# One attention-and-expert kernel: batch 0's token reads taken from the opening to mid-run, and the whole hand-written order of the work set anew

## The chip, the cores and the metric

The kernel runs on one core of a Trainium2 chip. The metric is the device time of one execution in microseconds (us). Three runs of the kernel before took 211.06, 211.47 and 211.60 us; their median, 211.47 us, is its time. A fourth run was profiled; every row quoted below comes from it.

## What is computed

Eight batches of tokens `x` (8 heads, 512 tokens, 64 features) and states (8 heads, 32 rows, 64 features) read each other, and the results go through one layer with a leaky activation. Cut from the reference:

```python
scores  = scale * x @ state.T            # tokens read states
a       = softmax(scores)                # over the 32 states
xread   = a @ state
scores2 = scale * state @ x.T            # states read tokens
a2      = softmax(scores2)               # over the 512 tokens
sread   = a2 @ x
y = concat([xread, sread])               # 8 x 544 rows of 512
h = y @ w_in                             # 512 -> 2048
g = maximum(h, 0) + alpha * minimum(h, 0)
out = g @ w_out                          # 4352 x 512, float32
```

## The kernel before

**The order.** No loop and no scheduler sets the order. One string, ORDER, lists tokens such as `F.1.4.5`, and each token calls one step. A step issues a few instructions, and every engine runs its instructions in the order in which the string brings them. What a step needs it waits for by semaphores. So a place in the string is a place in up to five queues at once: TensorE (PE), VectorE (DVE), ScalarE (ACT), GpSimd (POOL) and SyncE (SP), the last two of which issue the DMAs. A trailing number is one of the PSUM banks k0 to k5; scores and a few other results use a two-bank buffer, called "two" here. An engine letter (a, v, p) chooses ACT, DVE or POOL.

**Tokens read states, then the first matrix.** The weights `a` stay apart from the states: the states go through `w_in` at once (step m, L521: eight matmuls for each batch and 512 columns; mo, L545 and L547, brings the result to SBUF), and the transposed weights are multiplied by that (F, L570: two 128x512 matmuls fill one bank `h`; batch 0 has a few quarters f, L592). For batch b the weights come by this chain: scores sc (L314, PE), turned into blocks sb (L346, DVE), their maximum smax (L379, DVE), subtracted by ssh (L384, POOL), exponent sexp (L393, ACT), sum and reciprocal ssum (L400, L401, DVE), division snorm (L404, DVE, for batch 0 POOL), turned back wb (L412, DVE). Batch 0's weights come from a second set of scores with tokens in rows (tsc, L353) and are turned on PE (at, L365).

**The activation.** N (L623, ACT) reads the bank and writes the negative part; G (L626, DVE) reads both and writes `g` in half precision. The bank is free when G is done. A bank `h` thus takes PE, ACT and DVE in turn.

**The second matrix.** Batch 0 uses plain matmuls (S, L640; O, L657). Batches 1 to 7 and the state rows, called batch 8, use products of halves (P, L728, four 128x256 matmuls each) on sums of `w_out` (W, L683, POOL) and of `g` (U, L707, POOL or DVE); K (L744) keeps a product, Q (L759, L761) adds it and issues the output's DMA from SP.

**States read tokens.** From the same scores: the maximum tm (L424, DVE), its negative nb (L431 ACT or L433 DVE), two exponents te (L441, ACT), reciprocals tsum (L451, DVE). Two steps tn (L457 ACT or L459 POOL) divide the exponents, tt (L463) turns them by a DMA on SP (`e2T`), rd (L475, PE) multiplies them with `x`, rdo (L486, ACT) takes the reads out of PSUM. Four batches' reads are turned together (rt, L494) and later fill batch 8, whose first matrix is L579.

**Loads.** POOL's queue carries the four parts of `w_in` (wi, L207), the four of `w_out` (wo, L213), the states of batches 1 to 7 (lst, L201) and `x` of batches 1 to 7 (lx, L161), which casts to half precision; three buffers `xg` hold `x` in turn. Batch 0's `x` comes by SP in float32 and is cast (L172, L177); batch 0's states come by ACT in float32 (L185). `x` of batches 0 and 1 is turned on PE (xt, L299, out by xo, L304), that of the others by a DMA on SP (xd, L291, `xT`). Fills (Z, L232) are matmuls on a pattern, whose result nobody reads.

Of the kernel before, what the change touches and what calls it, by code (L numbers as in the profile page):

```python
# [8 lines left out]
F32 = mybir.dt.float32  # L9
F16 = mybir.dt.float16  # L10
# [7 lines left out]
Z.1.1 Z.2.1 stc.a cx.0.0.a stt.3 wi.0 sbd.0.a Z.4.1 cx.0.1.v xt.0.0.1.5 xo.0.0.1.a sbd.1.v xt.0.0.0.0 xo.0.0.0.v  # L18
tsc.0.1.1 lst cx.1.0.a lx.1 sto.a cx.1.1.v tsc.0.0 Z.2.1 wi.1 smax.0.0 xt.0.1.1.4 xo.0.1.1.v xt.0.1.0.5 wo.0 tsc.1.1.0
xo.0.1.0.a tsc.1.0 Z.2.1 m.0.0.3.4 ssh.v.0.0 sc.0.1 sexp.0.0 oma wi.2 mo.0.0.a.0 mo.0.0.a.1 Z.5.1 smax.0.1 ssum.0.0  # L20
snorm.p.0.0 ssh.v.0.1 str.0.1 sro.0.a sc.0.0 tm.0 Z.2.1 sexp.0.1 str.1.5 Z.3.1 at.0.4 ao.0.v nb.0.v ssum.0.1
xt.1.1.1.2 xo.1.1.1.v sro.1.a m.4.0.0.1 mo.4.0.v.0 te.0.1 te.0.0 xt.1.1.0.3 xo.1.1.0.a xt.1.0.1.4 f.0.1.0.5 mo.4.0.v.1
m.1.0 mo.1.0.v f.0.0.0.2 n.0.1.0 snorm.p.0.1 xt.1.0.0.0 at.1.1 ao.1.v n.0.0.0 xo.1.0.1.a g.0.1.0.0 g.0.0.0.1 m.0.1.3.1
xo.1.0.0.a sc.1 m.2.0.4.0 mo.0.1.a.1 mo.0.1.a.0 mo.2.0.a.0 g.0.0.0.0 S.0.2.0.1 mo.2.0.a.1 tm.1 sb.1 F.0.5.2 F.0.4.3
nb.1.a wo.1 g.0.1.0.1 wi.3 f.0.1.1.4 N.0.5 G.0.5 F.0.6.0 te.1.0 smax.1 N.0.4 S.0.2.1 G.0.4 F.0.7.5 te.1.1 f.0.0.1.2
m.0.2 N.0.6 n.0.1.1 G.0.6 g.0.1.1.1 mo.0.2.a g.0.1.1.0 wo.2 wo.3 tsum.0 S.0.1.2.3 S.0.2.2 F.0.11.0 N.0.7 G.0.7 ssh.p.1
n.0.0.1 F.0.10.4 g.0.0.1.0 g.0.0.1.1 S.0.1.1 N.0.11 G.0.11 sexp.1 ssum.1.5 m.0.3 mo.0.3.a S.0.2.3 S.0.1.3 S.0.1.0
m.1.1 N.0.10 G.0.10 tn.0.0.p mo.1.1.a tn.0.1.p tt.0 F.0.9.2 snorm.v.1 F.0.8.0 N.0.8 m.1.3 N.0.9 G.0.9 S.0.1.5 mo.1.3.a
W.1.0.p F.0.14.4 N.0.14 F.0.15.5 N.0.15 S.0.2.5 m.1.2 mo.1.2.a G.0.8 S.0.2.4 wb.1 lx.2 G.0.14 xd.2 F.0.13.2 N.0.13
# [12 lines left out]
N.2.8 G.2.8 N.2.1 F.2.13.4 K.1.2.a G.2.1 N.2.13 P.1.7.0.0.2 G.2.13 P.1.7.1.1 m.3.3.1.3 ssh.p.3 m.2.1 sexp.3 tn.2.1.a
tt.2 P.1.5.0.1 ssum.3.5 P.1.5.1.0 mo.3.3.a.0 tn.3.1.p tt.3 mo.3.3.a.1 mo.2.1.a P.1.5.1.1 P.1.7.1.0 snorm.v.3 P.1.7.0.1
P.1.5.0.0 K.1.4.a Q.1.1.1 F.2.14.4 N.2.14 G.2.14 m.4.2.1.3 sc.4 tm.4 U.1.4.1.p mo.4.2.a.0 mo.4.2.a.1 P.1.3.0.1
U.1.4.0.p P.1.3.1.0 W.4.0.p U.2.1.0.p P.1.3.0.0 m.4.1.5.1 mo.4.1.a.1 nb.4.v mo.4.1.a.0 rd.2.4 rd.3.3 P.1.4.0.1 F.2.7.1
rdo.3.a te.4.0 wb.3 sb.4 N.2.7 G.2.7 P.1.4.1.1 F.2.6.5 N.2.6 F.2.5.3 N.2.5 P.1.4.1.0 smax.4 rdo.2.a lx.5 P.1.3.1.1
Q.1.0.1.a G.2.6 U.2.2.0.p P.1.4.0.0 G.2.5 te.4.1 tsum.4 F.2.4.1 N.2.4 G.2.4 xd.5 P.2.2.1.1.4 Q.1.1.0 F.3.1.0 N.3.1
P.2.2.0.1 F.3.4.5 N.3.4 P.2.2.0.0 F.3.9.3 G.3.1 N.3.9 G.3.4 G.3.9 P.2.1.1.0.1 ssh.p.4 sexp.4 F.3.15.2 ssum.4.0
P.2.1.1.1 N.3.15 G.3.15 P.2.1.0.1 P.2.1.0.0 K.2.1.a snorm.v.4 rt.0.5 m.5.2 mo.5.2.a P.2.6.1.0 F.3.13.3 P.2.2.1.0
Q.2.0.0 P.2.6.0.0 U.2.1.1.p U.2.2.1.p U.2.4.1.p P.2.6.1.1 tn.4.1.a P.2.6.0.1 N.3.13 rto.0.a m.7.0.2.0 K.2.2.a  # L50
mo.7.0.a.0 sc.5 wb.4 U.2.3.1.p mo.7.0.a.1 F.3.6.5 N.3.6 F.3.11.4 F.3.12.2 N.3.11 P.2.5.0.1 tm.5 nb.5.a G.3.13 G.3.6
G.3.11 F.3.2.0 N.3.2 U.2.4.0.p G.3.2 N.3.12 G.3.12 P.2.5.1.0 P.2.5.0.0 P.2.5.1.1 K.2.4.a F.3.5.3 N.3.5 F.3.8.5 N.3.8
G.3.5 F.3.7.4 tn.4.0.p tt.4 N.3.7 G.3.7 P.2.3.0.0 F.3.14.0 N.3.14 F.3.3.2 N.3.3 P.2.3.0.1 lx.6 G.3.8 F.3.0.3 N.3.0
# [48 lines left out]
def kernel(  # L102
# [17 lines left out]
    nc = tc.nc  # L120
# [55 lines left out]
    def x0_cast(j, g, e):  # L176
        copier(e)(xgs[0][:, 4 * g : 4 * g + 4, j, :, :], x0s[j][:, 4 * g : 4 * g + 4, :, :])  # L177
# [635 lines left out]
```

## Time and profile before

| What | Before |
|---|---|
| median of three runs | 211.47 us (211.06 to 211.60) |
| the profiled run's own time | 210.96 us |
| its span, first to last instruction | 209.2 us |
| PE, DVE, ACT, POOL busy | 199.0, 182.0, 150.9, 165.6 us |
| granted PE clock | 1.00 |
| first matmul F of batch 1 | 33.69 us into the span |
| last product P begins, its four matmuls end | 204.43, about 205.3 us |

A "busy" matmul lasts longer in the rows than the time from its start to the next one's start, since matmuls are pipelined; the same holds, less, on DVE and ACT. So the cost of one instruction in a row of its kind is taken here from starts to starts, and called its pace. Names such as `h<-aT,m` read "out from in". "Landed" is when a DMA's data have arrived.

### The profile page before, as it was taken

How to read it: one execution, taken by the hardware profiler on the slowest of the kernel's cores; microseconds unless marked ns; L12 is line 12 of the kernel's file. 1: busy time of each engine (PE TensorE's matmuls, PEld its weight loads, DVE VectorE, ACT ScalarE, POOL GpSimd, SP SyncE). 2: the span in 40 equal slices, each digit the busy share in tenths (PEclk: the TensorE clock that was granted, in tenths of full speed). 3: DMA queues.
4: the chain of work that ended last, by engine and by line, in shares of the span. 5: the costliest groups of instructions: out<-in, count | busy, mean ns of one | idle time of the engine just before them, and what ended most of it. 6: DMA issues, size and time to landing. Idle time of an engine off the chain costs nothing.

```text
span 209.2 us, 5108 instructions
## 1 busy us (share of the span) xinstructions
PE 199.0 (95%) x2024; PEld 132.9 (64%) x2024; DVE 182.0 (87%) x275; ACT 150.9 (72%) x293; POOL 165.6 (79%) x105
## 2 busy tenths in 40 slices
PE   7787799999999999999999999999999999999993
PEld 2453333443667677666577776667778777788882
DVE  0899999999999999999999999999899868595750
ACT  3799998999999889998897748956876386423000
POOL 8244599899999999998999999897981999504640
PEclk9999999999999999999999999999999999999999
DMA  6999999698586698269981572034201111013142
GB/s 167 219 204 206 206 188 130 154 156 161 120 104 147 125 93 194 68 90 168 141 109 39 104 165 97 12 93 127 75 3 53 50 50 53 0 50 103 60 150 95
DMA packets 49992, 23.71 MB, mean 113 GB/s; under 512 B 34480, under 2 KB 49456, under 8 KB 49968
## 3 DMA queue, kind: packets, MB, share of 16 engines
q0 software_dynamic: 17792, 8.09, 30.1%
q1 hardware_dynamic: 31904, 15.22, 29.6%
q8 instruction: 16, 0.26, 0.5%
q10 hardware_dynamic: 272, 0.07, 0.1%
q14 instruction: 8, 0.07, 0.1%
HBM read 17.31 MB, written 8.91 MB: 125 GB/s over the span
## 4 chain that ended last, share of the span: by engine, by line
PE 61%; DMA 12%; DVE 11%; POOL 11%; issue 1%; ACT 0%; SPq 0%; POOLq 0%; DVEq 0%
PE px L728 19%; PE h L570 16%; PE pv L728 9%; POOL gsum L707 7%; DVE g L626 6%; PE py L728 6%; DMA w_in_sb<-in_moe_w_in_dram 5%; DMA st<-in_state_dram 4%; PE h L579 3%; PE o L640 2%; PE m_ps L521 2%; DMA xT<-xg 2%; DMA e2T<-e 2%; DVE oq L761 1%; DVE nb L424 1%
## 5 line engine op out<-in xcount | busy, mean ns | idle before, releaser
L626 DVE SCALAR_TENSOR_TENSOR g<-neg,oma_sb,h 128x512 f16<-128x512 f32 (+1 forms) x140 | 92.3, 707 | 7.4 <-ACT neg L623 6.8
L623 ACT ACTIVATE neg<-h 128x512 f32<-128x512 f32 (+1 forms) x140 | 75.1, 579 | 20.6 <-PE h L570 15.5
L570 PE MATMUL h<-aT,m 128*128 128x512 f16 x248 | 67.3, 379 | 0.2
L728 PEld LDWEIGHTS <-gsum 128*128 128x128 f16 x480 | 46.2, 98 | 13.0 <-issue 1.5
L728 PEld LDWEIGHTS <-g 128*128 128x128 f16 x360 | 35.1, 98 | 11.2 <-issue 0.9
L707 POOL TENSOR_TENSOR gsum<-g,g 128x1024 f16<-128x1024 f16 (+1 forms) x14 | 27.8, 1990 | 11.6 <-DVE g L626 7.2
L707 POOL TENSOR_TENSOR gsum<-gsum,g 128x1024 f16<-128x1024 f16 (+1 forms) x15 | 30.0, 2003 | 8.3 <-DVE gsum L707 7.5
L570 PEld LDWEIGHTS <-m 128*128 128x128 f16 x248 | 23.8, 98 | 16.1 <-issue 1.9
L728 PE MATMUL px<-ws,gsum 128*128 128x256 f16 x240 | 32.8, 273 | 0.0
L707 POOL TENSOR_TENSOR gsum<-g 128x1024 f16<-128x1024 f16 (+1 forms) x14 | 28.8, 2064 | 0.8 <-PE pv L728 0.8
L707 POOL TENSOR_TENSOR gsum<-g,gsum 128x1024 f16<-128x1024 f16 x12 | 25.4, 2130 | 0.2
L744 ACT COPY kept<-px 128x512 f32<-128x512 f32 (+1 forms) x20 | 11.5, 577 | 11.3 <-PE px L728 9.5
L547 ACT CAST m<-m_ps 128x512 f16<-128x512 f32 x33 | 18.0, 604 | 1.9 <-PE m_ps L521 1.7
L640 PE MATMUL o<-w_out_sb,g 128*128 128x512 f16 x64 | 17.5, 380 | 1.8 <-DVE g L626 1.0
L384 POOL TENSOR_TENSOR ts<-ts,mx 128x1024 f32<-128x1024 f32 x7 | 13.4, 1913 | 5.9 <-DVE mx L379 5.9
L728 PE MATMUL py<-w_out_sb,g 128*128 128x256 f16 x120 | 17.5, 273 | 0.1
L728 PE MATMUL px<-w_out_sb,g 128*128 128x256 f16 x120 | 16.7, 272 | 0.1
L728 PE MATMUL px<-w_out_sb,gsum 128*128 128x256 f16 x120 | 16.7, 273 | 0.0
L728 PE MATMUL pv<-ws,gsum 128*128 128x256 f16 x120 | 16.1, 273 | 0.0
L728 PE MATMUL pv<-ws,g 128*128 128x256 f16 x120 | 15.7, 273 | 0.0
L761 DVE TENSOR_TENSOR oq<-pv,kept 128x512 f32<-128x512 f32 (+1 forms) x16 | 10.4, 652 | 5.2 <-PE pv L728 4.8
L521 PE MATMUL m_ps<-w_in_sb,stT 64*32 64x512 f16 x256 | 12.6, 384 | 1.1 <-DMA w_in_sb<-in_moe_w_in_dram 0.4
(84 smaller groups left out, 253.6 us busy)
## 6 DMA issues: line engine op xcount, KB each, us to landing
out_dram<-oq SPq DMA_DIRECT2D x28, 256.0 KB, 2.7
xg<-in_x_dram POOLq DMA_DIRECT2D x7, 512.0 KB, 7.1
w_in_sb<-in_moe_w_in_dram POOLq DMA_DIRECT2D x4, 512.0 KB, 11.3
w_out_sb<-in_moe_w_out_dram POOLq DMA_DIRECT2D x4, 512.0 KB, 13.4
x<-in_x_dram SPq DMA_DIRECT2D x2, 512.0 KB, 5.0
out_dram<-osb SPq DMA_DIRECT2D x4, 256.0 KB, 2.7
out_dram<-oq SPq DMA_DIRECT2D x4, 128.0 KB, 2.1
st<-in_state_dram POOLq DMA_DIRECT2D x1, 224.0 KB, 7.5
```

Source lines behind the costliest of these rows:

```text
L384: engine(e).tensor_tensor(blocks(cols(live["ts", b], j, S)), blocks(scored(b, j)), over_blocks(cols(live["mx", b], j, S // N)), ALU.subtract,)
L521: nc.tensor.matmul(t[N * k : N * (k + 1), :], st_head(b, h)[64 * r : 64 * r + 64, :], w_in_sb[64 * r : 64 * r + 64, c, 512 * f : 512 * (f ...
L547: copier(e)(m_tile(b, f)[:, g, :], t[g])
L570: nc.tensor.matmul(h.rearrange("p (r j s) -> p r j s", r=2, j=2), ms[b, f][:, g, 128 * j : 128 * (j + 1)], weights(b, g), start=(g == 0), ...
L579: nc.tensor.matmul(h, w_in_sb[:, c, 128 * jc : 128 * (jc + 1)], XS[:, c].rearrange("p q n b -> p (q n b)"), start=(c == 0), stop=(c == n_c ...
L623: nc.scalar.activation(neg, h, RELU, bias=0.0, scale=-1.0)
L626: nc.vector.scalar_tensor_tensor(g_tile(b, jc), negs.pop((b, jc)), oma_sb[:, jc : jc + 1], hs.pop((b, jc)), ALU.mult, ALU.add,)
L640: nc.tensor.matmul(outs[b, q], g_tile(b, jc)[:, 128 * q : 128 * (q + 1)], w_out_sb[:, jc, :], start=not begun and jc == 2 * jc2, stop=left ...
L707: engine(e).tensor_tensor(t, x(), y(), op)
L728: nc.tensor.matmul(pbanks[b, name][:, i, :], of(b, c)[:, j, 128 * i : 128 * (i + 1)], moving[:, 4 * c + j, :], start=not begun and j == 0, ...
L744: copier(e)(t, pbanks[b, "x"])
L761: nc.vector.tensor_tensor(osb, pbanks[b, name], kept[b, add], ALU.add)
```

## The change

1. Batch 0's `x` is kept as `xg_first` and `xT_first` for its token scores alone. The full scores, their maximum, exponents, transposition and reads of batch 0 leave the opening; a second load of `x[0]` (lx.0) and a DMA transposition (xd.0) give them their data in mid-run, between batch 4's and batch 5's.
2. The exponents are no longer divided before the transposition: tn is gone (10 POOL, 6 ACT instructions). rdo scales instead, one copy for each of two halves with its own reciprocal (15 ACT, 1 DVE, each 128x64 instead of 8 ACT copies of 128x128). The reciprocals get four buffers instead of two.
3. Batch 1's states come in float32 by SP, and go the way that batch 0's did; the load lst holds 768 columns instead of 896.
4. nb is on ACT in all eight batches (four before). The fills' pattern has 256 columns, used twice.
5. Every token has a new place. The lines move by three to six.

The core of the diff:

```diff
-                live["xT", 0][:, h, j, :],
+                live["xT", "first"][:, h, j, :],
-    nc.scalar.dma_start(st0_32, rows[:n0, :].rearrange("(g p) d -> p g d", p=128))
+    for b in range(2):
+        (nc.sync if b else nc.scalar).dma_start(
+            st0_32[b], rows[n0 * b : n0 * (b + 1), :].rearrange("(g p) d -> p g d", p=128)
+        )
-        nc.gpsimd.dma_start(st, rows[n0:, :].rearrange("(p j) d -> p j d", j=n_j))
+        nc.gpsimd.dma_start(st, rows[2 * n0 :, :].rearrange("(p j) d -> p j d", j=n_j))
-            live["r2", b] = att.tile([128, 2], F32, name=f"r2_{b}", tag="r2", bufs=2)
+            live["r2", b] = att.tile([128, 2], F32, name=f"r2_{b}", tag="r2", bufs=4)
-    def token_norm(b, g, e):
-        e2 = live["e2", b][:, g, :, :]
-        r2 = live["r2", b][:, g : g + 1]
-        if e == "a":
-            nc.scalar.mul(e2, e2, r2)
-        else:
-            nc.gpsimd.tensor_scalar(e2, e2, r2, 1.0, ALU.mult, ALU.mult)
-    def state_reads_out(b, e):
-        copier(e)(reads[:, b % 4], live.pop(("sr", b)))
+    def state_reads_out(b, g, e):
+        to, t, r2 = reads[:, b % 4, g, :], live["sr", b][:, g, :], live["r2", b][:, g : g + 1]
+        if e == "a":
+            nc.scalar.mul(to, t, r2)
+        else:
+            nc.vector.tensor_scalar_mul(to, t, r2)
 ORDER = """
...
+rd.0.5 tsum.0 rdo.0.0.a rdo.0.1.a rd.4.0 lx.6 xd.6 m.5.1
...
```

**The loads in the opening.** POOL's queue of before, from its tenth row: the weights' parts, the states `st`, batch 1's `xg`, and two divisions `an` for batch 0's weights.

```order
10 L207 DMA w_in_sb<-in_moe_w_in_dram 128x4x512
11 L201 DMA st<-in_state_dram 128x896
12 L161 DMA xg_142<-in_x_dram 128x8x256
13 L207 DMA w_in_sb<-in_moe_w_in_dram 128x4x512
14 L213 DMA w_out_sb<-in_moe_w_out_dram 128x4x512
15 L207 DMA w_in_sb<-in_moe_w_in_dram 128x4x512
16 L404 TENSOR_TENSOR an_156<-ts_153,r_0_155 128x512 x2
17 L213 DMA w_out_sb<-in_moe_w_out_dram 128x4x512
```

The same place now:

```order
10 L210 DMA w_in_sb<-in_moe_w_in_dram 128x4x512 x3
11 L414 TENSOR_TENSOR an_151<-ts_148,r_0_150 128x512
12 L161 DMA xg_335<-in_x_dram 128x8x256
13 L210 DMA w_in_sb<-in_moe_w_in_dram 128x4x512
14 L204 DMA st<-in_state_dram 128x768
15 L216 DMA w_out_sb<-in_moe_w_out_dram 128x4x512 x4
```

Three parts of `w_in` now go ahead of batch 1's `x`, the states behind the fourth, and `w_out` last; POOL makes one division `an` instead of two (DVE makes the other).

**DVE between the token maximum of batch 1 and what stands ahead of it.** DVE's queue of before, from its 16th row. `nb_258` is batch 0's maximum tm.0, `nb_414` batch 1's tm.1, `ts_416` batch 1's blocks sb.1; the `m` are products of the states with `w_in`.

```order
16 L424 TENSOR_REDUCE nb_258<-sc_194 128x2
17 L368 COPY aT_157<-at_ps_280 128x512
18 L433 TENSOR_SCALAR nb_258<-nb_258 128x2
19 L400 TENSOR_REDUCE r_0_155<-ts_153 128x16
20 L401 RECIPROCAL r_0_155<-r_0_155 128x16
21 L304 COPY xT_294<-xT_ps_1_1_289 128x4x128
22 L547 CAST m_0_307<-m_ps_0_0_297 128x512
23 L547 CAST m_0_307<-m_ps_0_1_298 128x512
24 L545 CAST m_0_339<-m_ps_0_330 128x1024
25 L368 COPY aT_157<-at_ps_354 128x512
28 L424 TENSOR_REDUCE nb_414<-sc_377 128x2
29 L346 STREAM_TRANSPOSE ts_416<-sc_377 128x1024
```

Now, from the 33rd row (`nb_446` is tm.1, `ts_490` sb.1, `mx_491` smax.1; the `g` are batch 0's):

```order
33 L632 SCALAR_TENSOR_TENSOR g_1_319<-neg_4_369,oma_sb,h_4_312 128x512
34 L314 COPY xT_349<-xT_ps_0_1_375 128x4x128
35 L632 SCALAR_TENSOR_TENSOR g_2_331<-neg_11_390,oma_sb,h_11_352 128x512
36 L632 SCALAR_TENSOR_TENSOR g_1_319<-neg_6_393,oma_sb,h_6_366 128x512
37 L617 SCALAR_TENSOR_TENSOR g_0_286<-neg_1_1_342,oma_sb,h_1_1_337 128x2x128
38 L434 TENSOR_REDUCE nb_446<-sc_429 128x2
39 L356 STREAM_TRANSPOSE ts_490<-sc_429 128x1024
40 L632 SCALAR_TENSOR_TENSOR g_1_319<-neg_7_454,oma_sb,h_7_448 128x512
41 L389 TENSOR_REDUCE mx_491<-ts_490 128x32
```

Batch 0's maximum and three casts of `m` have left this stretch; all eight quarters `g` of batch 0 and six of its whole `g` now come ahead of tm.1, and six `g` between it and the turning back wb.1.

**Where batch 6's `x` is loaded.** POOL's queue of before around that load (`xg_1679`), with the semaphores that each row waits for:

```order
58 L459 TENSOR_SCALAR e_4_1365<-e_4_1365,r_4_1366 128x512 [waits DMAHW1_49,Activation_49]
59 L161 DMA xg_1679<-in_x_dram 128x16x128 [waits DMAHW4_49,DMASW3_49]
60 L707 TENSOR_TENSOR gsum_3_0_1710<-g_0_1042 128x1024
```

The same place now (`xg_1657`):

```order
50 L713 TENSOR_TENSOR gsum_3_0_1539<-g_0_1057 128x1024
51 L161 DMA xg_1657<-in_x_dram 128x16x128 [waits DMAHW3_49,DMASW5_49,PE_49]
52 L713 TENSOR_TENSOR gsum_1_0_1692<-g_0_1324,g_2_1407 128x1024 [waits DVE_49]
```

The load now also waits for PE: the buffer is that of batch 4's `x`, whose reads rd.4 are the last PE work on it. On PE, rd.0 and rd.4, some products and F, the scores of batch 5 and more follow up to the scores of batch 6, which need this load and its transposition.

203 lines of the change are left out of this document (105 added, 98 removed).

## The prediction

> **What bounds the kernel now.** First the page: busy times, and the lines of forty slices.
>
> ```profile
> PE 199.0 (95%) x2024; PEld 132.9 (64%) x2024; DVE 182.0 (87%) x275; ACT 150.9 (72%) x293; POOL 165.6 (79%) x105
> PE   7787799999999999999999999999999999999993
> DVE  0899999999999999999999999999899868595750
> GB/s 167 219 204 206 206 188 130 154 156 161 120 104 147 125 93 194 68 90 168 141 109 39 104 165 97 12 93 127 75 3 53 50 50 53 0 50 103 60 150 95
> ```
>
> PE is busy nearly without a gap from slice 6 on; only the first 30 us show holes. DVE is full beside it from 10 to 140 us. Next, the windows (columns: length, then busy time and instructions of PE, PEld, DVE, ACT, POOL, clock, DMA).
>
> ```profile
> 10.00:20.00 10.00, 7.90 (x132) 4.46 (x132) 9.83 (x19) 9.44 (x19) 5.08 (x6) 1.00 1.30 205
> 60.00:70.00 10.00, 10.00 (x117) 6.87 (x116) 9.85 (x16) 9.71 (x17) 10.00 (x7) 1.00 0.69 132
> ```
>
> From 10 to 20 us DVE and ACT are both full while PE is not: DVE and ACT bound the opening. At 60 us PE, DVE and ACT are all full. Last, the chain of work that ended last, some pieces of it:
>
> ```profile
> 36.50 4.28 DMA xT<-xg
> ...
> 54.00 1.16 POOL xg L161
> ...
> 88.01 1.29 PE h L570 x6
> ...
> 99.75 0.56 PE m_ps L521 x16
> ...
> 103.81 0.22 PE sc L314 x16
> ...
> 118.59 0.34 issue
> ...
> 125.83 5.26 DVE g L626 x8
> ...
> 138.40 1.21 issue
> ...
> 199.62 3.06 PE px L728 x28
> ```
>
> They give the paces: 1.29/6 = 0.215 us for a 128x512 matmul, 3.06/28 = 0.109 for 128x256, 0.56/16 = 0.035 for a state matmul, 0.22 for a batch's scores, 5.26/8 = 0.66 for a G. And they say that the end is PE's from 142 us on, but that between 116 and 142 us the chain runs through DVE, with waits of 0.34 and 1.21 us. A bank `h` is held until its G, so where PE's order runs ahead of DVE's, PE waits for DVE. So the time is: when PE gets going, its work from there, and what it later loses to DVE or to a transfer.
>
> **The opening: 1.3 us gained.** PE gets going with the first F of batch 1, when the weights have been turned back:
>
> ```profile
> 18.15 1.22 DVE L424 TENSOR_REDUCE nb<-sc 128x2 f32<-128x1024 f32 x1
> 19.28 1.24 DVE L346 STREAM_TRANSPOSE ts<-sc 128x1024 f32<-128x1024 f32 x1
> 21.46 1.21 DVE L379 TENSOR_REDUCE mx<-ts 128x32 f32<-128x1024 f32 x1
> 27.13 1.23 DVE L400 TENSOR_REDUCE r<-ts 128x32 f32<-128x1024 f32 x1
> 28.66 0.69 DVE L626 SCALAR_TENSOR_TENSOR g<-neg,oma_sb,h 128x512 f16<-128x512 f32 x1
> 29.27 1.21 DVE L404 TENSOR_TENSOR an<-ts,r 128x1024 f16<-128x1024 f32 x1
> 32.18 1.24 DVE L412 STREAM_TRANSPOSE aT<-an 128x1024 f16<-128x1024 f16 x1
> 33.69 1.03 PE L570 MATMUL h<-aT,m 128*128 128x512 f16 x4
> ```
>
> Now this chain starts later and is shorter. It starts with the scores sc.1, which use the buffer "two", and so wait for the last of batch 0's `m`, mo.0.3. That is ACT's, behind a full queue:
>
> ```profile
> 15.30 1.31 ACT L607 ACTIVATE neg<-h 128x512 f32<-128x512 f32 x2
> 17.56 2.05 ACT L547 CAST m<-m_ps 128x512 f16<-128x512 f32 x4
> 26.05 1.05 ACT L393 ACTIVATE ts<-ts 128x1024 f32<-128x1024 f32 x1
> 28.80 1.01 ACT L545 CAST m<-m_ps 128x1024 f16<-128x1024 f32 x1 [0.23 <-PE m_ps L521]
> ```
>
> Before, the first negative part of batch 0 began at 15.30; two copies of stT for other batches and four exponents stood ahead of it on ACT, and batch 0's maximum ahead of the weights' sum on DVE. These are gone from there; I let it begin at 14.0 us (bounds 13.6 and 14.8). From it to mo.0.3 ACT has eighteen rows: three casts of 1024 at 0.9 (1.01 less the overlap), ten N or halves of `m` at 0.5 (2.05 for four), five smaller copies included among these at most at 0.5, 8.6 us in sum. So mo.0.3 ends at 22.6, sc.1 (0.22) and a hand-over of 0.3 let tm.1 start at 23.1, five later than the 18.15 of before. From there DVE has tm (19.28 - 18.15 = 1.13), sb 1.17, one G 0.66, smax 1.13: it is 27.2. POOL's ssh takes 1.91 by the row below, sexp 1.05, that is 30.2; DVE meanwhile does five G, until 30.5, and so doesn't wait. Then ssum 1.53 (28.66 - 27.13), snorm 1.14, wb 1.16: 34.3. F follows 0.27 after wb, as in 32.18 + 1.24 = 33.42 to 33.69: 34.6; with 0.3 for hand-overs, **34.9 us**, 1.2 later than before.
>
> ```profile
> L384 POOL TENSOR_TENSOR ts<-ts,mx 128x1024 f32<-128x1024 f32 x7 | 13.4, 1913 | 5.9 <-DVE mx L379 5.9
> ```
>
> By the two orders, PE has 24 matmuls S, 22 of F and 80 of `m` ahead of that F before, and now 32, 24 and 96: ten of 0.215 and sixteen of 0.035 more, 2.7 us; less batch 0's scores, 0.22, which go behind it. So 2.5 us less stand after this F, which starts 1.2 later: a gain of **1.3 us** (bounds 0.6 and 1.8, by the ends of the start on ACT and with or without the hand-overs).
>
> **The middle: 0.7 lost.** I added the paces along both orders, for PE and DVE, and looked where a PE row needs most DVE work beyond what PE itself has done by then. Before, this need is 7.4 us at F.1.9 (needs G.1.14), 7.9 at m.3.3 (needs G.2.8), and about the same up to 140 us. Now it is 4.8 at F.1.4, and rises to 6.0 between 85 and 104 us of PE work. PE's loss is DVE's own loss, the need, and a hand-over; the need grows by 0.5 there and by 1.2 here, so **0.7 us** of the gain goes again (bounds 0 and 1.2, as DVE gains or loses on the way). DVE has 2.2 us less to do: nb leaves it, four rows of the kind below, 0.55 each.
>
> ```profile
> L433 DVE TENSOR_SCALAR nb<-nb 128x2 f32<-128x2 f32 x4 | 2.2, 546 | 0.1
> L431 ACT ACTIVATE nb<-nb 128x2 f32<-128x2 f32 x4 | 0.9, 223 | 0.2 <-DVE nb L424 0.2
> L486 ACT CAST XS<-sr_ps 128x128 f16<-128x128 f32 x8 | 2.3, 282 | 0.9 <-PE sr_ps L475 0.8
> L457 ACT ACTIVATE e<-e,r 128x512 f16<-128x512 f16 x6 | 4.4, 735 | 0.1
> L459 POOL TENSOR_SCALAR e<-e,r 128x512 f16<-128x512 f16 x10 | 6.9, 694 | 0.5 <-ACT neg L623 0.4
> ```
>
> **Divisions and reads: nothing.** ACT loses six divisions (4.4 us) and eight copies (2.3), and gains four nb (0.9) and fifteen scaled copies. A scaled copy isn't in the trace; between the 223 ns of a 128x2 row and the 282 ns of twice its size I take 0.25, 3.8 us in all. ACT's sum falls by 2.0 us; POOL's by 6.9. Both sums are off the end's path in mid-run (ACT is busy 72% of the span), so the cover for the extra waits of rdo on the reciprocals is ACT's idle time; where ACT is full (60 to 70 us), each further 0.25 delays an N, and DVE behind it, by as much.
>
> **Late: 1.25 gained.** By the same sums PE loses 1.87 us between 95 and 145 us before, 0.75 of it around the wait of 1.21 us at 138.40, since it stands at the limit of DVE all the way. Now the need falls from 6.0 to 5.1, 4.5 and 3.7 after 104 us, so DVE can lose one to two us there unseen. I take **1.25** (bounds 0.75 and 1.87).
>
> **Batch 6's load: 0.7 lost.** The transfers' medians from issue to landing, and the spread of the transpositions:
>
> ```profile
> xg<-in_x_dram POOLq DMA_DIRECT2D x7, 512.0 KB, 7.1
> DMA to landing us min/median/max: 4.3/4.3/5.4
> DMA to landing us min/median/max: 3.0/3.6/6.5
> ```
>
> (the last two of `xT` and of `e2T`, in this order). The new load lx.6 can't be issued before rd.4 has ended. From there load and transposition take 7.1 + 4.3 and a hand-over of 0.2, 11.6 us. PE has 10.45 us of work between rd.4 and the scores sc.6: 1.15 us of standing. Part falls where PE would wait for DVE anyway: **0.7** (bounds 0 and 3.05, the case B below). The Trainium skill, "DMA: Bandwidth & Descriptors", section "Latency and other measured facts", gives a DMA transposition 261 GB/s; by it, as an estimate, 512 KB would take 2.0 us, and the stall and its 0.7 us would vanish. The trace's 4.3 us from issue to landing speaks against it, and the measurement decides.
>
> The second load of `x[0]` costs POOL one issue, 1.16 us as at 54.00, which the 6.9 us of divisions more than pay, and its transposition lies long ahead of sc.0. Its price is in that no queue stands then; if its cover goes, it is a load as above, in front of sc.0. The tail is the same: the last product at 204.43 and an output.
>
> **Sum.** -1.3 + 0.7 - 1.25 + 0.7 = -1.15 us on the profiled run's own 210.96, so 209.8. That run is 0.5 below the median of the three; a median is likelier to be as that one: 211.47 - 1.15 = **210.3 us**. About 0.3%, 0.63 us, is what a measurement can tell here.
>
> **Rivals.** **C, the loads hold the opening.** The queue moves 205 GB/s, 512 KB in 2.55 us. Batch 1's `x` now comes behind three parts of `w_in`, and the fourth, which mo.0.3 needs, behind that: I reckon it landed at 20.3 us: the first part at 9.3, as before (issued at 1.92, 7.4 to landing, the minimum below), then four pieces of 2.55 and the small ones. Before it landed at 26.54 (15.97 + 10.57).
>
> ```profile
> 1.92 0.92 POOL w_in_sb L207
> ...
> 15.97 10.57 DMA w_in_sb<-in_moe_w_in_dram
> ```
>
> ```profile
> DMA to landing us min/median/max: 7.4/11.3/15.6
> ```
>
> Its matmuls are wanted at 21.5, so the cover is 1.2 us; past that each us is one. With a queue of 2.5 us more (one part more ahead of it) the term of 1.3 is gone: 211.5 us, the same as before. For it: all parts come in one row of transfers; against it: the part goes out earlier than before.
>
> **B, batch 6's load in the long form, slower.** In before the first load in mid-run was issued at 28.44 and its transposition began at 36.50, 8.06 later.
>
> ```profile
> 28.44 1.24 POOL L161 DMA_DIRECT2D xg<-in_x_dram  x1
> ```
>
> That and a transposition of 5.4 make 13.5 against 10.45: PE stands 3.05 instead of 0.7, and the time is 212.7. The place is sc.6. It decides from load and transposition of 12.8 us on, where the sum's gain is used up. For it: the long `e2T` (6.5, against 3.0) lie beside a load in flight, and here `e2T` of batch 0 and the load of batch 5 stand near; against it: five of six `xT` took 4.3. The same skill page, section "SWDGE vs HWDGE vs iDMA", says that the software and the hardware queue feed different internal queues of each DMA engine, which it serves in turn; the 3.0 and 6.5 agree with it, and by it a transposition beside a load would take longer, as in B.
>
> **D, PE and DVE hold each other, slower.** Besides PE's need there is DVE's: it can't run ahead of what PE has done. Before, 8.05 to 9.0 us of DVE work were allowed ahead, where 7.9 were needed; now 5.3 to 6.4, where up to 6.0 are needed. In such a narrow window each late row on one costs both. With a wait of 0.34 as at 118.59, seven times (once for each batch from 1 on), 2.4 us are lost: 212.7. For it: windows just as narrow as before already cost those waits; against it: the sum counts the growth of the same kind.
>
> **Chances.** The forecast 0.50, C 0.20, B 0.15, D 0.15. So faster 0.50, the same 0.20, slower 0.30. The range reaches from the opening and the late term at their better ends without a stall at sc.6 in part (208.8) to B and D with a little of C (213.4).
>
> **What would show it.** Right: tm.1 at about 23.1 and the first F of batch 1 at about 34.9 us; the fourth part of `w_in` landed by 21 us; no wait of DVE over 1 us near 140 us; PE's idle time ahead of sc.6 under 1 us. Wrong: that F after 36 us (C, where `w_in` releases PE; or ACT's queue longer than 8.6); over 2 us ahead of sc.6 with `xT` as releaser (B); many waits of PE for G and of DVE for N between 40 and 110 us (D).

## The result, and the profile after

The changed kernel took 218.78 us in the median of six runs (216.13 to 220.68), the kernel before 211.30 us in six (211.04 to 211.60). The ratio is 1.031, with a 95% interval of 1.025 to 1.037: 3% slower, where 0.55% faster was forecast. (This ratio leaves out the two slowest runs, 220.10 and 220.68 us, which lie over 1.5% above the fastest.) The profiled run took 220.10 us, at the upper end of the kernel's runs; a second profile, of a run of 219.12 us, shows two of its three main waits (below, the last experiment).

The page after, its span, PE's busy time, PE's slices and the granted clock:

```profile
span 218.3 us, 5047 instructions
PE 202.7 (93%) x2008; PEld 133.8 (61%) x2008; DVE 181.3 (83%) x272; ACT 150.4 (69%) x302; POOL 156.4 (72%) x94
PE   7788899949999999999999599999999999999993
PEclk9999999997999999999999999999999999999999
```

The opening looks no worse than before. New are two holes in mid-run, in slices 9 and 23, and a clock below full in slice 10, right behind the first. The windows, with the columns as in the prediction:

```profile
40.00:50.00 10.00, 7.15 (x52) 2.81 (x49) 7.27 (x11) 5.88 (x12) 8.93 (x5) 0.90 1.13 188
50.00:60.00 10.00, 9.56 (x92) 3.92 (x90) 8.86 (x12) 8.70 (x19) 7.29 (x4) 0.93 0.91 92
120.00:130.00 10.00, 7.79 (x130) 5.93 (x128) 9.12 (x12) 5.63 (x12) 10.00 (x6) 1.00 0.60 121
```

From 40 to 50 us PE, DVE and ACT are each idle for 2.7 to 4.1 us, so none of them is the limit there. PE's waits name what they wait for (who waited, for whom, total us, times, longest):

```profile
PE sr_ps L477 <- DMA e2T<-e: 3.2, 2, 2.2
PE sc L324 <- DMA xT<-xg: 3.0, 2, 2.8
```

Both are DMA transpositions: `xT` of batch 2 ahead of the scores sc.2, and `e2T` ahead of the reads of batches 2 and 6. Here are two places on PE's timeline, the first F of batch 1, which the prediction places, and sc.2:

```profile
38.34 1.47 PE L576 MATMUL h<-aT,m 128*128 128x512 f16 x6 [0.15 <-DVE r L461]
...
47.84 0.48 PE L324 MATMUL sc<-xT,stT 64*32 64x256 f16 x16 [2.85 <-DMA xT<-xg]
```

That F starts at 38.34 us; forecast were 34.9. Why so late is on POOL's timeline:

```profile
1.64 2.41 POOL L210 DMA_DIRECT2D w_in_sb<-in_moe_w_in_dram  x3
13.19 1.05 POOL L414 TENSOR_TENSOR an<-ts,r 128x512 f16<-128x512 f32 x1 [9.13 <-DVE r L411]
14.18 0.95 POOL L161 DMA_DIRECT2D xg<-in_x_dram  x1
15.12 0.76 POOL L210 DMA_DIRECT2D w_in_sb<-in_moe_w_in_dram  x1
...
27.79 2.12 POOL L689 TENSOR_TENSOR ws<-w_out_sb 128x1024 f16<-128x1024 f16 x1 [8.39 <-DMA w_out_sb<-in_moe_w_out_dram]
29.86 1.20 POOL L161 DMA_DIRECT2D xg<-in_x_dram  x1
...
39.30 1.18 POOL L161 DMA_DIRECT2D xg<-in_x_dram  x1
```

POOL issues three parts of `w_in` and then comes to the division `an`, for which it waits 9.13 us. Batch 1's `x`, the fourth part of `w_in`, the states and all of `w_out` are queued behind it. Their issues begin at 14.18 us, when the third part is about to land (14.81) and nothing else is under way in that queue. Before, `x` had been issued at 3.4 us. Once more, batch 2's load (29.86) stands behind a sum `ws` that waits 8.39 us for `w_out`, and it lands at 40.76. Batch 1's subtraction ssh stands behind the same two: it starts at 31.08 us, 0.8 after its maximum was there. Then batch 3's load (39.30) and the transposition of batch 2 (40.91) start 1.6 us apart. The chain after shows how long the transpositions of batches 2 and 6 are; the two that stand in the chain before took 4.28 (`xT` of batch 2) and 3.52 us (an `e2T`):

```profile
40.91 6.89 DMA xT<-xg
...
54.28 6.25 DMA e2T<-e
...
119.94 4.35 DMA e2T<-e
```

### The profile page after: what moved, and what is told of

It reads as the page before. It is cut to its first block, busy times and chain, and to the rows that moved or that the text cites. A ratio compares the mean times of both kernels' runs of the same rounds, so it can differ in the third digit from the quotient of the medians.

```text
span 218.3 us, 5047 instructions
## 1 busy us (share of the span) xinstructions
PE 202.7 (93%) x2008; PEld 133.8 (61%) x2008; DVE 181.3 (83%) x272; ACT 150.4 (69%) x302; POOL 156.4 (72%) x94
## 4 chain that ended last, share of the span: by engine, by line
PE 59%; DMA 19%; DVE 12%; issue 3%; POOL 3%; ACT 3%; SPq 0%; DVEq 0%; ACTq 0%; POOLq 0%
PE px L734 18%; PE h L576 16%; PE pv L734 10%; DMA w_out_sb<-in_moe_w_out_dram 5%; DVE g L632 5%; DMA xT<-xg 5%; PE py L734 5%; DMA e2T<-e 5%; DMA st<-in_state_dram 4%; PE h L585 3%; PE o L646 2%; PE m_ps L527 2%; DVE r L410 1%; DVE an L414 1%; DVE aT L422 1%
## 5 line engine op out<-in xcount | busy, mean ns | idle before, releaser
L629 ACT ACTIVATE neg<-h 128x512 f32<-128x512 f32 (+1 forms) x140 | 74.0, 580 | 13.1 <-PE h L576 9.9
L576 PE MATMUL h<-aT,m 128*128 128x512 f16 x248 | 64.4, 382 | 0.5 <-DVE aT L378 0.2
L734 PEld LDWEIGHTS <-gsum 128*128 128x128 f16 x480 | 46.5, 98 | 10.3 <-issue 0.9
L713 POOL TENSOR_TENSOR gsum<-g,g 128x1024 f16<-128x1024 f16 (+1 forms) x14 | 28.8, 2058 | 24.4 <-DVE g L632 20.6
L734 PE MATMUL px<-ws,gsum 128*128 128x256 f16 x240 | 30.5, 273 | 0.0
L750 ACT COPY kept<-px 128x512 f32<-128x512 f32 (+1 forms) x22 | 12.6, 573 | 25.1 <-PE px L734 25.0
L713 POOL TENSOR_TENSOR gsum<-gsum,g 128x1024 f16<-128x1024 f16 (+1 forms) x14 | 27.8, 1990 | 0.6
L713 POOL TENSOR_TENSOR gsum<-g 128x1024 f16<-128x1024 f16 (+1 forms) x14 | 27.8, 1993 | 0.0
L734 PE MATMUL py<-w_out_sb,g 128*128 128x256 f16 x120 | 16.4, 273 | 0.0
L734 PE MATMUL px<-w_out_sb,gsum 128*128 128x256 f16 x120 | 16.1, 273 | 0.0
L689 POOL TENSOR_TENSOR ws<-w_out_sb 128x1024 f16<-128x1024 f16 x4 | 8.5, 2128 | 8.4 <-DMA w_out_sb<-in_moe_w_out_dram 8.4
```

The source lines that it names most:

```text
L576: nc.tensor.matmul(h.rearrange("p (r j s) -> p r j s", r=2, j=2), ms[b, f][:, g, 128 * j : 128 * (j + 1)], weights(b, g), start=(g == 0), ...
L629: nc.scalar.activation(neg, h, RELU, bias=0.0, scale=-1.0)
L689: engine(e).tensor_tensor(ws[i][:, rows, :], w_halves[a][:, rows, :], (ws[b] if b in ws else w_halves[b])[:, rows, :], ALU.subtract,)
L713: engine(e).tensor_tensor(t, x(), y(), op)
L734: nc.tensor.matmul(pbanks[b, name][:, i, :], of(b, c)[:, j, 128 * i : 128 * (i + 1)], moving[:, 4 * c + j, :], start=not begun and j == 0, ...
L750: copier(e)(t, pbanks[b, "x"])
```

## The experiments

Two theories stood at first: **O**, that the loads issued late in the opening are the loss, and **M**, the prediction's rival D, that PE and DVE hold each other in mid-run. A third came out of the first runs: **K**, that a transposition on SP and a load in POOL's queue make each other long when they are in flight together, and that the in-order queues of SP and POOL pass this on. Each edit moves tokens of ORDER, so "in front of" is a place in that string. Medians stand with the range of the runs; ratios are to the kernel before, run on the same chip.

**e1, the loads ahead of the division.**

```diff
 wi.2
+lx.1 wi.3 lst wo.0 wo.2
 ...
 snorm.p.0.0
 ...
```

The same five tokens are gone from their later places.

> The changed kernel with five DMA issues (batch 1's x, the last part of w_in, the states, two parts of w_out) moved ahead of the division an on POOL, which had waited there until 13.19 us. Theory O (the opening's loads, issued 10 us late, cost most of the loss): batch 1's x lands at about 17.5 us instead of 21.4, the first F of batch 1 starts at 35.5 to 36.5 us instead of 38.3, the scores sc.2 wait under 2 us, and the time falls to 214 to 215.5 us. Rival M (the mid-run part costs it: the second load of batch 0's x makes transpositions long, and PE and DVE hold each other): the first F comes earlier, but the time stays at 217 or above.

Measured: 214.87 us (212.86 to 215.95), ratio 1.015 (1.007 to 1.022). Batch 1's `x` landed at 17.54 us, that F started at 36.91 (35.5 to 36.5 was expected), and PE no longer waited at sc.2: batch 3's load, whose place is unchanged, was issued (37.80) 2.4 us behind batch 2's transposition (35.36, 4.29 us). 3.9 us came from five places in POOL's queue. O gives this; M doesn't. But only 1.4 us of it are that F's; the rest was won at sc.2 and rd.2.

**e2, the cast and turning of batch 1's states behind batch 0's `x`.**

```diff
 cx.1.1.a
-stc.1.a
 Z.5.1 cx.1.0.a
-stt.1.4
 xt.0.1.0.1 xo.0.1.0.v sexp.0.0 xt.0.1.1.0 xo.0.1.1.v
+stc.1.a stt.1.4
```

> The changed kernel with the cast and transposition of batch 1's first states moved behind the second half of batch 0's x, on ACT and PE; the loads stay where they are. Theory O: PE's wait of 1.8 us for the states' load goes, the division an starts at about 11.8 instead of 13.2 us, the loads behind it and the first F of batch 1 come 1.3 us earlier, and the time falls by 1 to 1.5 us. Rival M: no change that can be measured, within 0.7 us of the changed kernel.

Measured: 220.49 us (219.71 to 221.97), ratio 1.043 (1.037 to 1.049): slower, against all theories. Yet its first step did more than was expected: the division began 2.3 us sooner, and that F 2.8 sooner, at 35.50. What was won was lost at once:

```profile
35.50 1.41 PE h L576 x6
...
36.91 8.73 DMA xT<-xg
```

```profile
PE sc L324 <- DMA xT<-xg: 6.1, 2, 3.5
```

The first fence is the chain, the second PE's waits. Batch 3's load was issued at 36.41, half a us ahead of batch 2's transposition at 36.91; the load then took 9.02 us and the transposition 8.73. This is where K comes from.

**e3, the kernel before with its loads late.**

```diff
-lst cx.1.0.a lx.1 sto.a
+lst cx.1.0.a sto.a
 ...
-wo.0
 ...
 snorm.p.0.0
+lx.1 wo.0
```

> The kernel before with two DMA issues (batch 1's x, one part of w_out) moved behind the first division an on POOL, as in the change. Theory O: batch 1's x lands at about 17 instead of 13.0 us, the token maximum of batch 1 starts some 2 to 3 us later, the time rises to 212.5 to 214.5 us. Rival M: the opening has slack, the time stays within 0.7 us of 211.3.

Measured: 219.31 us (218.83 to 219.94), ratio 1.037 (1.033 to 1.042). The direction is O's, the size far more:

```profile
11.31 1.05 POOL L404 TENSOR_TENSOR an<-ts,r 128x512 f16<-128x512 f32 x1 [6.43 <-DVE r L401]
12.30 0.95 POOL L161 DMA_DIRECT2D xg<-in_x_dram  x1
```

```profile
PE xT_ps L299 <- DMA xg<-in_x_dram: 8.1, 1, 8.1
```

`x` landed at 20.84 instead of 13.03, and in the order of before PE turns batch 1's `x` ahead of batch 0's first matmuls, so all of it became time: 7.8 us of load, 8.1 of kernel. In the order of before, two loads behind one waiting instruction are enough for a loss as large as the change's. That the two sizes agree is chance: in the changed kernel that F is 3.0 us later than in e14, and the rest is lost in mid-run.

**e4, the moves of e1 and e2 and batch 2's load** (also `lx.2` in front of `W.1.0.p`).

> Both moves on the changed kernel (e1 and e2), and batch 2's load ahead of the first sum of w_out on POOL. Theory O: the first F of batch 1 at 34 to 35 us, no wait over 1 us at the scores sc.2, time 211 to 213 us. Rival M: 216 us or more, the waits for transpositions in mid-run as long as in the changed kernel.

Measured: 216.04 us (213.64 to 219.39), ratio 1.022 (1.012 to 1.031). That F came at 35.35 us, near O's 34 to 35, but the time missed O's range and reached M's mark of 216: sc.2 waited again. The releaser is a transfer and not DVE: batch 3's load (36.23) and batch 2's transposition (36.04) now meet:

```profile
44.80 0.41 PE L324 MATMUL sc<-xT,stT 64*32 64x256 f16 x16 [2.81 <-DMA xT<-xg]
```

**e5, e6, e7: the meetings parted.** e5 is e4 with `lx.3` behind `W.1.1.p`; e6 also has `tt.5` behind `tt.6`; e7 has these two on the changed kernel without e4's moves.

> The kernel of three moves (e4) with one more: batch 3's load behind two more sums of w_out on POOL, so that it is issued at about 40.5 us instead of 36.2, after batch 2's transposition has landed. Theory K (a DMA transposition on SP and a load in POOL's queue that are in flight together make each other long): the transposition takes 4.3 us instead of 8.7, the wait of 2.8 us at the scores sc.2 goes, the time falls by 2.5 to 4.5 us, to 211 to 213 us, with less scatter. Rival M (PE and DVE hold each other; the wait only moves): less than 1 us gained.

> The same and batch 5's token transposition moved behind batch 6's on SP, so that it no longer lies beside batch 7's load. Theory K: batch 7's load takes 6 to 7 us instead of 9.6, batch 6's transposed weights land 2 us earlier, the wait of 1.5 us at the reads rd.6 shrinks to under 0.5; the time is 208.5 to 210.5 us, below the kernel before. Rival M: 212 us or more, the gain of the opening given back by waits between PE and DVE.

> The changed kernel with only these two later places (batch 3's load, batch 5's token transposition); its opening with the late loads stays. Theory K with O: the opening still costs its 2 to 3 us (first F of batch 1 at 38.3 us), the meetings 4 to 5; the time is 212.5 to 214.5 us. If the opening alone is the cause: 217 us or more. If the meetings alone are: 210 to 211 us.

Measured: e5 221.99 us (218.56 to 224.23; too scattered for a ratio), e6 220.27 (218.65 to 221.16; ratio 1.043, 1.038 to 1.047), e7 221.78 (220.40 to 224.16; 1.049, 1.045 to 1.052). All three missed K's ranges by 7 us and more, and by their times alone the rivals' marks were met: M's in e5 and e6, that of the opening alone in e7. But where the edit acted, K was right. On PE's timeline of e5, sc.2 waits for nothing (e4 above: 2.81), and batch 2's transposition took 4.28 us against 8.72, with nothing changed but the place of one load:

```profile
42.67 0.41 PE L324 MATMUL sc<-xT,stT 64*32 64x256 f16 x16
```

Then POOL's timeline of e5, and SP's:

```profile
41.16 1.18 POOL L161 DMA_DIRECT2D xg<-in_x_dram  x1
...
48.76 1.18 POOL L161 DMA_DIRECT2D xg<-in_x_dram  x1
```

```profile
48.56 1.99 SPq L299 DMA_TRANSPOSE xT<-xg  x1
50.65 2.33 SPq L465 DMA_TRANSPOSE e2T<-e  x1
```

Batch 3's load now lands at 48.42; its transposition (48.56) meets batch 4's load (48.76), and batch 2's `e2T` stands behind it on SP though its exponents were long done. They took 7.79 and 7.43 us, against 4.93 and 3.04 in e4, and the reads rd.2 stood:

```profile
PE sr_ps L477 <- DMA e2T<-e: 5.3, 1, 5.3
```

The wait had been handed on by one batch; e6 and e7 show the same, no wait at sc.2 and 4.91 and 5.17 us at rd.2. e6's second edit gained nothing at its place either: batch 7's load still took 10.25 us, so batch 5's `e2T` alone was not what made it long.

**e8, a part of the change alone: before with scaled reads** (the steps tn gone, rdo in two scaled copies, four buffers for the reciprocals).

> The kernel before with one part of the change alone: no division of the exponents, the reads scaled in two copies per batch as they leave PSUM. All theories: no cost of its own, within 0.6 us of the kernel before. If the scaled copies are the loss: 213 us or more.

Measured: 214.43 us (213.03 to 215.29), ratio 1.014 (1.009 to 1.019). Not free, and over the mark of 213 for the scaled copies. Yet the loss does not stand where the copies do. Here are a wait on PE's timeline and, in the second fence, the landing times of the tile `e2T`:

```profile
26.17 1.87 PE L643 MATMUL o<-w_out_sb,g 128*128 128x512 f16 x4 [2.96 <-DMA w_out_sb<-in_moe_w_out_dram]
```

```profile
DMA to landing us min/median/max: 3.0/4.2/11.6
```

Without the divisions batch 0's `e2T` was issued at 15.09 us instead of 26.42, in the midst of the weights, took 11.6 us, and a part of `w_out` landed 2.1 us later (26.04 against 23.93). Set beside before, PE is 0.1 us late ahead of this wait, 3.7 late behind it and its low clock (0.66 from 25 to 30 us), 3.3 at sc.2 (44.11 against 40.82), and 3.9 at the end of the span. All scaled copies come after sc.2, so at most 0.6 us is left to their charge. The POOL work that the change removed had kept this transposition out of the loads.

**e9 and e11: apart from batch to batch.** e11 is e5 with `lx.4 xd.4` behind `U.1.2.1.p`. e9 has also `xd.3` behind `tt.2`, and `P.3.3.1.1 P.3.3.1.0` in front of `rd.6.3`.

> The same without the change of order on SP and without the two products: batch 3's and 4's loads later only. Theory K: batch 3's transposition takes 4.3 to 5 us instead of 7.8, batch 2's token transposition lands at about 53.5 instead of 58 us, the wait at rd.2 falls from 5.3 to about 1, rd.6 keeps its 1.5 to 2; time 211 to 213 us. Rival (the wait at rd.2 is SP's order alone, not the meeting): batch 2's token transposition still takes 7 us, the wait stays over 4, time 217 or more.

> The kernel of three moves with batch 3's load later (as e5), batch 2's token transposition ahead of batch 3's x on SP, batch 4's load behind two sums of g on POOL, and two products ahead of the reads rd.6 on PE. Theory K (load and transposition in flight together are both long, in-order queues pass it on): no wait of PE over 1 us at sc.2, rd.2, sc.3, under 1 at rd.6; 209 to 211 us, the gain that the blind sum saw. Rival M (PE and DVE hold each other): 212.5 us or more although these waits are gone.

Measured: e11 213.66 us (213.17 to 215.81), ratio 1.013 (1.008 to 1.017); e9 213.66 (211.29 to 217.66), 1.0075 (1.0045 to 1.0104). In e11 the same `e2T` that took 7.43 us in e5 takes

```profile
49.80 3.46 DMA e2T<-e
```

and `xT` of batch 3 takes 4.35 instead of 7.79; only batch 4's load and its own transposition were moved. That settles K against SP's order alone, and 8 us fall. e9 then has no wait of PE over 1 us for a transfer in its profiled run, at 211.29 the fastest of twelve; but the median lies above the 209 to 211 that was expected, and above M's mark of 212.5, and other runs reach 217.7. So e9 alone doesn't rule M out. Batch 7's load (98.15, 9.91 us) beside batch 6's transposition was left.

**e10, the changed kernel with fourteen fills in front of sc.2** (`Z.5.14`).

> The changed kernel with fourteen fill matmuls (3.0 us at full rate) ahead of the scores sc.2, where PE stood 2.85 us. Theory G (the granted clock falls after such a wait, 0.71 from 46 to 51 us, so that the wait costs about 1.5 us more than it lasts): the clock stays 1.00 there and the time falls by 1 to 2 us. If the low clock costs nothing: the same time, or 0.2 to 0.5 longer.

Measured: 216.54 us (215.74 to 217.86), ratio 1.026 (1.022 to 1.030); the changed kernel's interval, 1.025 to 1.037, overlaps it. First the windows of the changed kernel, then those of e10:

```profile
45.00:50.00 5.00, 2.16 (x28) 0.68 (x28) 2.27 (x3) 1.33 (x3) 4.03 (x2) 0.81 1.18 271
50.00:55.00 5.00, 5.00 (x52) 2.26 (x51) 4.14 (x6) 3.80 (x11) 3.02 (x2) 0.85 0.57 48
```

```profile
45.00:50.00 5.00, 5.00 (x76) 2.13 (x75) 2.09 (x2) 1.83 (x5) 2.49 (x2) 1.00 1.22 223
50.00:55.00 5.00, 5.00 (x31) 2.10 (x30) 5.00 (x8) 4.81 (x12) 3.45 (x3) 1.00 0.36 70
```

In the changed kernel the granted clock is 0.81 and 0.85 in the ten us around the wait of 2.85 us; with work that keeps PE busy through the wait it is 1.00 in e10's profile. The price is read from the starts: from sc.2 to rd.2 the changed kernel takes 12.73 us, 1.01 of them a wait for `e2T`, and e4 and e10, with the same PE order there and a full clock, 10.13; so 1.6 us are the clock's. It doesn't follow each such wait: in e4 PE waited 2.81 us, and its clock stayed at 1.00. The Trainium skill, "TensorE: Matmul & The Clock Gate", section "Why this matters for your kernels", warns of idle gaps of more than about 3 us between bursts of matmuls. These traces agree, and go further: all seven waits of PE for a transfer of 2.96 us or more were followed by a drop, but so were six of the eleven between 1.5 and 2.9 us, the shortest of 1.87 (e11).

**e12 and e13: the last meeting, and the second load.** e12 is e9 with `tt.5` behind `tt.6` and `lx.7` behind `U.3.2.1.p`. e13 leaves the second load of batch 0's `x` and its transposition out.

> The kernel kept apart (e9) with batch 7's load behind one more sum of g on POOL (issued when batch 6's transposition has landed) and batch 5's token transposition behind batch 6's on SP. Theory K: batch 7's load takes 6 to 7.5 us instead of 9.9, the wait of 0.8 us and the half-rate products after it at the reads rd.6 go, the time falls by 1 to 2 us against e9, to 210 to 212 us in the median and 209 to 210 at best. Rival (the load is long for the outputs' sake, not the transpositions'): still 9 us or more, and no gain.

> The same kernel with batch 0's reads taken from batch 4's x, so that the second load of batch 0's x and its transposition are left out (and the rows of batch 0's states hold other values). If the second load costs time by its own transfers (theory S): 0.7 us or more faster than e12. Theory K: the second load meets no transfer that PE waits for, so within 0.5 us of e12.

Measured: e12 211.64 us (210.68 to 214.05), ratio 1.000 (0.997 to 1.003); e13 211.61 (210.59 to 214.25), 1.001 (0.999 to 1.003). Batch 7's load takes 7.18 us instead of 9.91, and the runs scatter over 3.4 us instead of 6.4. With the meetings gone, the second load costs nothing that can be told (the intervals leave some 0.6 us). In e12, as already in e9, the longest `xT` is 4.8 us, where it had been 6.9 in the changed kernel:

```profile
DMA to landing us min/median/max: 4.3/4.3/4.8
```

**e14, two places more**: `lx.0 xd.0` behind `U.1.4.0.p`, and `m.7.0.4.1 mo.7.0.a.1` in front of the two products of e9.

> The kernel e12 with two more places: the second load of batch 0's x behind one more sum of g on POOL (the products of batch 1 had waited 0.7 us for that sum), and the state products m.7.0 ahead of the two products that were put before rd.6 (P.4.1 had waited 0.8 us for ACT). Theory K with these as the only other losses: 1 to 1.5 us faster than e12, 210 to 210.8 us, ahead of the kernel before by 0.3 to 0.6%. Rival (the waits only move to the next one): within 0.5 us of e12.

Measured: 210.73 us (209.98 to 212.12), ratio 0.997 (0.995 to 0.9995). That is far below the changed kernel, and 0.3% below the kernel before, at the edge of what can be told. The profiled run took 210.07:

```profile
span 208.3 us, 5048 instructions
PE 198.9 (95%) x2008; PEld 132.1 (63%) x2008; DVE 180.5 (87%) x272; ACT 150.1 (72%) x302; POOL 156.4 (75%) x94
```

```profile
35.34 1.47 PE L576 MATMUL h<-aT,m 128*128 128x512 f16 x6
...
41.92 0.41 PE L324 MATMUL sc<-xT,stT 64*32 64x256 f16 x16
```

No wait of PE for a DMA of over 0.1 us is left in it. Batch 0's second transposition, beside batch 5's load, still takes 6.32 us, but nothing waits for it. PE's work is that of the changed kernel, as are the steps on DVE and ACT; twenty tokens of ORDER have other places, and 8 us are gone.

**e15, the changed kernel again.**

> The changed kernel once more, for another profile: the wait of about 2 to 3 us at sc.2, the waits at the reads rd.2 and rd.6, and batch 2's transposition of 6 to 9 us show again; 216 to 220 us.

Measured: 219.23 us (219.12 and 219.33). PE waits 2.3 us at sc.2 for `xT` (6.44 us long, issued at 39.70; batch 3's load at 37.86) and 2.3 at rd.6 for `e2T`; rd.2 did not wait this time. The clock fell behind both waits (0.56 and 0.58 from 122 to 126 us); in the first profile it stayed at 1.00 behind the wait of 2.21 us at rd.6. Two of the three places repeat, and their sizes vary by a us or two from run to run.

PE's starts at five places, from the timelines. The kernels have one PE order but for the states' transposition in the opening; in e14 the state products m.7.0 and two products P are moved ahead of rd.6:

| | first F of batch 1 | sc.2 | rd.2 | sc.6 | rd.6 | span |
|---|---|---|---|---|---|---|
| changed | 38.34 | 47.84 | 60.57 | 109.42 | 124.33 | 218.3 |
| e2 | 35.50 | 45.68 | 58.38 | 109.65 | 124.19 | 218.2 |
| e1 | 36.91 | 43.49 | 53.61 | 102.49 | 117.11 | 211.1 |
| e4 | 35.35 | 44.80 | 54.93 | 103.64 | 117.87 | 211.9 |
| e5 | 36.09 | 42.67 | 58.12 | 111.72 | 126.10 | 220.1 |
| e14 | 35.34 | 41.92 | 52.05 | 101.11 | 115.40 | 208.3 |

Read along a row: e2 starts F three us sooner than the changed kernel and has lost them by sc.6. Read down: between that F and sc.2 PE needs 6.58 us in e1, e5 and e14 and 9.45 to 10.2 in the other three, and the difference is one meeting.

## Why the prediction was wrong, point by point

**What bounds the kernel** held: PE, with DVE beside it. But the transfers were counted as cover only, and they are what decided.

**The opening** is the step that failed first; two waits were missing from it. Once both are mended (e4, e14) the F starts at 35.35 and 35.34, against 34.9. The first is in how the loads were reckoned: "the first part at 9.3, as before ... then four pieces of 2.55". That is a queue that never runs dry. The row `11 L414 ... an_151` ahead of `12 L161` stood in the quoted order, and what is queued behind a waiting instruction on its engine was not asked. The fourth part of `w_in` landed at 23.89 us instead of 20.3 (20.68 in e14), and batch 1's `x` at 21.37 instead of the 17.7 that this implies. The second had no term at all: batch 1's states, now by SP beside `x` and `w_in`, took 7.86 us to land, and PE and ACT held batch 0's second half, and the division on POOL, behind them. For that F the second weighs more: tm.1 started at 26.15 us in the changed kernel, at 25.36 with the loads moved (e1), at 23.96 with the states' turn moved (e2), at 23.80 with both (e4). The forecast of 23.1 let ACT begin batch 0's negative parts at 14.0; they began at 17.13, and at 15.03 in e14. From there ACT's queue to mo.0.3 was right in its end, partly by luck: 22.91 in e14 against 22.6, but in fourteen rows and 7.9 us, where eighteen rows and 8.6 were counted, and the terms given for these add up to as much as 10.2.

**Batch 6's load** had the right mechanism, rival B's, in the wrong place, and this is the step that cost most. A load and a transposition in their long form were costed once, at sc.6. There PE waited 0.16 us in the changed kernel (the load took 6.22, not 7.1), though 2.52 in e2 and 3.55 in e5, near B's 3.05. The long form came instead at sc.2, rd.2 and rd.6, for which the sum has no term. The lengths were taken as constants (7.1 and 4.3) with a rare long form; they depend on what else is in flight, 4.28 or 8.72 for the same transposition (e5, e4). Already in the kernel before, four of the six `xT` took 4.3 to 4.4, not five; the others took 4.50 and 5.36. The Trainium skill, "DMA: Bandwidth & Descriptors", section "SWDGE vs HWDGE vs iDMA", says that each DMA engine serves the software and the hardware queue in turn. The long transpositions agree with it; that one kept its 4.30 us beside a load that took 9.91 (e9) doesn't follow from it, and no run here shows why. And the price of a wait was too low wherever the clock fell (e10). In the profiled run, 10.3 us above the 209.8 that were forecast for it, that F's 3.4 us, the waits of 2.85, 1.01 and 2.21 us and the clock's 1.6 add up to 11.1, so no large loss is left unnamed.

**The middle and the late term** held, as far as e14 can tell. By sums of paces over the rows of its trace (estimates, good to some tenths), PE of e14 loses 2.1 us from that F to sc.5, against 1.5 before (0.5 given back, forecast 0.7), and 1.4 from there to the last product, against 1.8 (0.4 gained; forecast, with batch 6's load, 0.55). In sum e14's span is 0.9 us under that of before, and its median 0.55, where 1.15 was forecast for the change.

**Divisions and reads: nothing.** e14 has all the scaled copies and no loss left to put down to them, and its batch 0 transposes in mid-run. As a part alone the change costs 3 us (e8), by what the removed work had kept apart.

**The second load: nothing.** Right where the transfers are kept apart (e13); in the changed kernel itself it was not tried.

**The rivals.** C came near: it named the order of the loads, but saw 1.2 us of cover, where the fourth part of `w_in` landed 2.4 us after the 21.5 at which it was wanted, and ended at 211.5. PE, late itself, waited 0.09 us for it. D is refuted for this order: with the waits for transfers gone PE and DVE give up about as much as before. The range ended at 213.4 since each rival was one mechanism once; in the run a late opening and meetings at three places came together.

What stays open: which of its meetings the changed kernel would keep with other loads late or early is not derived from a rule here, only seen run by run; and e12 to e14 keep transfers apart by places in a string, with a slack of some tenths of a us (e14's load 3 was issued at 40.41, batch 2's transposition landed at 40.48).

## What to carry to other kernels

Where an order is written by hand, read each in-order queue for the DMA issues behind the first instruction that waits, and follow each to its reader; a load's place in the queue is worth as much as a place on the bounding engine. Before moving a load, look at what transposition is in flight at its new time, and whether removed work had kept two transfers apart. And count a PE wait of 2 to 3 us at up to 1.6 us more: the clock fell behind some of them here, and behind all that were longer.

## What the runs showed of the hardware

- A 512 KB DMA transposition on SP (`xT`) that met no load took 4.25 to 4.4 us at best, and up to 6.1 with outputs or another transposition of SP's in flight. A 512 KB load on POOL's queue that met no transposition took 5.9 to 7.3.
- Which of two transfers becomes long depends on which comes first. An `xT` issued 1.3 to 2.8 us behind a load took 5.6 to 9.0 us; within half a us of one, 7.7 to 8.7. Where the load was issued 1.2 to 1.7 us behind the `xT` (eleven cases), the load took 9.6 to 11.0 us, and nine of the eleven `xT` only 4.3 to 4.6; a load issued 2.4 us behind lengthened neither (e1: 4.29 and 6.51).
- The same holds for batch 2's `e2T` and batch 4's load: 5.71 to 6.25 us where the load was issued 0.07 to 0.5 us ahead of it (e15, e2, the changed kernel), 3.04 where it was issued 1.0 us or more behind (e4, e10, e1). Among the weights an `e2T` took 11.6 us (e8).
- The granted clock fell, to 0.50 to 0.56 in the lowest window of 2 us, behind some PE waits: after 2.85 us in the changed kernel and 2.27 and 2.28 in e15, but not after 2.21 in the changed kernel or 2.81 in e4. From sc.2 to rd.2 that cost 1.6 us.
